# Seven unread matmuls before the first scores, a last product bank by bank with its copy on two engines, and a new issue order

## The chip, the core and the metric

One core of a Trainium2 chip runs the whole kernel. The metric is device time in microseconds of one launch; three runs of the kernel before were timed, and one more execution was profiled.

## What is computed

An attention with pooled keys and values is followed by a gated feed-forward layer. Eight batches of eight heads, 576 positions and head width 64 give 4,608 tokens of width 512; the feed-forward layer has 1,536 hidden columns.

```
k_p, v_p = mean of 8 neighbouring rows of k, v          # 72 keys
attn = softmax(q @ k_p.T / sqrt(64)) ; x = attn @ v_p
out  = (sigmoid(x @ w_gate) * (x @ w_val)) @ w_out
```

## The kernel before

The tokens go through in nine blocks of 512 columns (`BT`). Block 0 goes alone through `first_pass` (L1147); the other eight go in four pairs, and each pair of blocks is multiplied by the weights in seven products of half matrices (a Strassen scheme, `SLOTS`, `product`) instead of eight, first for gate and value (`hidden`), then for the output (`second_sums`, L1069). An operand that needs more than the fast matmul's precision is split into a high and a low part, so that one product is three matmuls (high by high, high by low, low by high).

**Where the order comes from.** No engine runs in the order in which the functions are written. Every call is recorded in `Book` (L283) as a unit, and units that belong together are grouped by `book.unit()`. At the end, L1512 to L1515 issue the recorded units in the order of a table of numbers, `LATER` (L112), one number for each of some 3,800 units. That table alone sets what stands behind what on TensorE (PE), VectorE (DVE), ScalarE (ACT), GpSimd (POOL) and in the queue of transfers (SP). Waits follow from the data and the buffers.

**The start.** `first` (L1165) issues the loads of block 0: keys `k0` to `k3` and queries `q0` to `q3` (one for each pair of heads), the constants, a matrix of ones for summing the values, and the values. POOL zeroes the five key tiles `kbd` (L350 and L356). DVE sums the keys of a pair over eight neighbours (`keys`, L1224), ACT places them in `kbd` (`place_keys`), PE makes the scores (`score_matmuls`, L662), four matmuls for a pair of heads; each is two rows of the trace, because both operands are full 32-bit values. DVE then takes the maximum (`maximum`) and subtracts it (`exps`), ACT takes the exponential, DVE sums, normalises, and PE transposes. The scores rotate through two PSUM banks, tags `sc` and `tp`, and others. DVE also makes a rounded copy `identr` of the identity out of the constants.

**The middle.** Block 0 and the weights' conversion overlap. A weight load (`fetch`, 1,024 KB from `in_wgv`, twelve of them) is turned into 32-bit numbers by ACT (two steps), DVE (two steps), and split by ACT and DVE into `parts` (`to_f32`, L384). PE then works through `chain` products of these parts and `acc` sums.

**The end.** `second_sums` runs 21 units of twelve matmuls (L1091). The last unit, product 4 of the last quarter, adds to two PSUM banks, `c` = 0 and 1: for `k` = 0 three matmuls into bank 0 and three into bank 1, then the same for `k` = 1 (L1105). `result` (L1073) then copies each bank to SBUF in two halves by ACT, and SP sends each half off with a transfer of its own.

Of the kernel before, what the change touches and what calls it, by code (L numbers as in the profile page):

```python
# [11 lines left out]
F32 = mybir.dt.float32  # L12
# [7 lines left out]
P = 128  # L20
# [309 lines left out]
def attention_then_ffn(ctx: ExitStack, tc: tile.TileContext, qT, kT, vm, vr, vn, sums8, wgv, wo, const, out, outT):  # L330
# [738 lines left out]
    def second_sums(n, last, build, later):  # L1069
# [3 lines left out]
        def result(side, half, c, bank, add):  # L1073
# [6 lines left out]
            if last and side and add is None:  # L1080
                for k in (0, BT // 2):
                    nc.scalar.copy(t[:, k:k + BT // 2], bank[:, k:k + BT // 2])
                    nc.sync.dma_start(outT[r:r + P, a + k:a + k + BT // 2], t[:, k:k + BT // 2])
# [486 lines left out]
```

## Time and profile before

| what | value |
|---|---|
| runs | 906.82, 908.58, 909.71 us; median 908.58 |
| profiled execution | 906.58 us, of which the span of the core's instructions is 904.8 |
| PE busy | 891.4 us, 4,148 rows |
| DVE, ACT, POOL busy | 657.4, 544.5, 200.0 us |
| bytes moved | 237.56 MB, mean 263 GB/s |

"Busy" is the time in which an engine has an instruction under way; PE's rows overlap, and a row's length is longer than the distance to the next. The distance is read from the start of one row to the start of the next, or from the length of a merged row and its count.

### The profile page before, as it was taken

How to read it: one execution, taken by the hardware profiler on the slowest of the kernel's cores; microseconds unless marked ns; L12 is line 12 of the kernel's file. 1: busy time of each engine (PE TensorE's matmuls, PEld its weight loads, DVE VectorE, ACT ScalarE, POOL GpSimd, SP SyncE). 2: the span in 40 equal slices, each digit the busy share in tenths (PEclk: the TensorE clock that was granted, in tenths of full speed). 3: DMA queues.
4: the chain of work that ended last, by engine and by line, in shares of the span. 5: the costliest groups of instructions: out<-in, count | busy, mean ns of one | idle time of the engine just before them, and what ended most of it. 6: DMA issues, size and time to landing. Idle time of an engine off the chain costs nothing.

```text
span 904.8 us, 12625 instructions
## 1 busy us (share of the span) xinstructions
PE 891.4 (99%) x4148; PEld 732.7 (81%) x4148; DVE 657.4 (73%) x1038; ACT 544.5 (60%) x1110; POOL 200.0 (22%) x369
## 2 busy tenths in 40 slices
PE   6999999999999999999999999999999999999998
PEld 5788878888888888888888888888888888888886
DVE  7989888889899999756668796355589552224863
ACT  5998998788978476545375555445365552224352
POOL 2422101012164235443443104132213000000000
PEclk9999999999999999999999999999999999999999
DMA  9899888889999888787987877676747776645554
GB/s 337 309 326 336 301 335 298 298 285 338 320 324 316 276 287 286 237 299 259 308 276 237 244 273 264 229 268 194 264 122 252 245 249 207 228 167 204 192 169 143
DMA packets 100433, 237.56 MB, mean 263 GB/s; under 512 B 13872, under 2 KB 34992, under 8 KB 98832
## 3 DMA queue, kind: packets, MB, share of 16 engines
q1 hardware_dynamic: 85328, 203.97, 66.6%
q0 software_dynamic: 15040, 32.79, 10.4%
q8 instruction: 33, 0.54, 0.2%
q14 instruction: 32, 0.26, 0.1%
HBM read 176.02 MB, written 60.69 MB: 262 GB/s over the span
## 4 chain that ended last, share of the span: by engine, by line
PE 81%; ACT 2%; DVE 1%; issue 0%; ACTq 0%
PE chain L317 50%; PE acc L317 25%; PE av L317 3%; PE sc L317 3%; ACT hs L317 0%; DVE s L317 0%; DVE hs L317 0%; PE tp L317 0%; DVE h L317 0%; ACT e L317 0%; ACT L317 0%; ACT raw_o L317 0%; DVE w_o L317 0%; ACT w_o L317 0%; ACT oparts L317 0%
## 5 line engine op out<-in xcount | busy, mean ns | idle before, releaser
L317 PE MATMUL chain<-xo,parts 128*128 128x512 f32 x2316 | 544.1, 392 | 0.5 <-ACT xs L317 0.5
L317 PEld LDWEIGHTS chain<-xo,parts 128*128 128x128 f32 x2316 | 430.7, 188 | 93.3 <-issue 1.0
L317 PE MATMUL acc<-hs,oparts 128*128 128x512 f32 x1008 | 237.0, 391 | 0.2 <-issue 0.2
L317 PEld LDWEIGHTS acc<-hs,oparts 128*128 128x128 f32 x1008 | 188.1, 188 | 40.6 <-DVE hs L317 1.2
L317 POOL DMA_DIRECT2D turned<-turn x240 | 131.7, 551 | 214.3 <-DVE turn L317 184.3
L317 DVE TENSOR_TENSOR y<-chain,sV 128x512 f32<-128x512 f32 x46 | 31.1, 686 | 69.6 <-PE chain L317 54.7
L317 ACT CAST hs<-h 128x1024 fp32r<-128x1024 f32 x52 | 54.3, 1051 | 27.2 <-PE acc L317 22.4
L317 DVE TENSOR_TENSOR hs<-h,hs 128x1024 fp32r<-128x1024 f32 x52 | 63.0, 1217 | 10.5 <-ACT hs L317 10.3
L317 ACT COPY chain<-chain 128x512 f32<-128x512 f32 x46 | 26.5, 577 | 52.8 <-PE chain L317 45.8
L317 DVE TENSOR_TENSOR y<-chain,sG 128x512 f32<-128x512 f32 x46 | 31.2, 682 | 34.2 <-PE chain L317 23.4
L317 ACT CAST hs<-s 128x1024 fp32r<-128x1024 f32 x36 | 37.5, 1050 | 28.5 <-DVE s L317 13.0
L317 DVE TENSOR_TENSOR hs<-s,hs 128x1024 fp32r<-128x1024 f32 x36 | 43.8, 1218 | 11.1 <-ACT hs L317 10.9
L317 ACT COPY sG<-chain 128x512 f32<-128x512 f32 x46 | 26.6, 584 | 41.0 <-PE chain L317 39.4
L317 ACT ACT_TABLE_LOAD x37 | 47.5, 1283 | 0.6
L317 ACT COPY sV<-chain 128x512 f32<-128x512 f32 x46 | 26.7, 584 | 34.0 <-PE chain L317 32.7
L317 ACT ACTIVATE gate<-chain 128x512 f32<-128x512 f32 x46 | 26.9, 594 | 31.8 <-PE chain L317 29.4
L317 DVE TENSOR_TENSOR h<-chain,gate 128x512 f32<-128x512 f32 x46 | 30.7, 679 | 20.1 <-PE chain L317 20.0
L317 PE MATMUL sc<-kbd,raw 128*128 128x144 f32 (+1 forms) x262 | 41.4, 297 | 0.3 <-ACT pr L317 0.2
L317 PEld LDWEIGHTS sc<-kbd,raw 128*128 128x128 f32 (+1 forms) x262 | 33.5, 176 | 8.6 <-issue 2.8
L317 ACT ACTIVATE gate<-y 128x512 f32<-128x512 f32 x46 | 28.9, 632 | 17.0 <-DVE y L317 16.8
L317 PE MATMUL acc<-oparts,hs 128*128 128x512 f32 x144 | 38.7, 402 | 0.0
L317 DVE TENSOR_REDUCE m<-sc 128x4 f32<-128x288 f32 x48 | 21.7, 452 | 17.5 <-PE sc L317 17.2
(210 smaller groups left out, 1099.9 us busy)
## 6 DMA issues: line engine op xcount, KB each, us to landing
oparts<-keptS SPq DMA_DIRECT2D x48, 512.0 KB, 4.7
oparts<-keptO SPq DMA_DIRECT2D x72, 256.0 KB, 4.7
raw<-in_wgv SPq DMA_DIRECT2D x12, 1024.0 KB, 8.1
out<-o SPq DMA_DIRECT2D x34, 256.0 KB, 3.8
raw<-in_kT SPq DMA_DIRECT2D x28, 288.0 KB, 5.0
raw<-in_qT SPq DMA_DIRECT2D x29, 256.0 KB, 4.9
raw<-in_vm SPq DMA_DIRECT2D x24, 256.0 KB, 5.5
raw_o<-in_wo SPq DMA_DIRECT2D x12, 512.0 KB, 8.5
```

The costliest lines, as they stand in the source:

```text
L317: return self._book.take(lambda: f(*args, **named))
```

## The change

1. In `first_pass`, seven matmuls of 128 by 144 with the last key tile (zeroed by POOL, not yet filled) as both operands, into a PSUM tile `idle` that nothing reads.
2. In the last unit of the last pair, bank 0 gets its six matmuls first, then bank 1 its six.
3. In the last `result`, bank 0 is copied whole by ACT and sent with one transfer. Of bank 1, ACT copies the first half and sends it from its own queue, and DVE copies the second half, which SP sends.
4. A new table `LATER`, for all units.

```diff
 LATER = """
-5 4 3 6 0 10 2 7 24 13 17 19 20 8 26 12 27 18 16 30 9 22 21 75 25 34 36 35 46 32 1 44 39 54 38 40 11 29 47 28 51 15 31
...
+6 4 5 0 11 7 2 3 21 18 8 27 28 14 31 20 25 1 19 35 9 13 36 22 23 17 40 48 39 10 26 37 45 76 66 33 32 47 53 67 12 41 30
...
@@ result @@
-            if last and side and add is None:
-                for k in (0, BT // 2):
-                    nc.scalar.copy(t[:, k:k + BT // 2], bank[:, k:k + BT // 2])
-                    nc.sync.dma_start(outT[r:r + P, a + k:a + k + BT // 2], t[:, k:k + BT // 2])
+            if last and side and add is None and c:
+                x, y = slice(0, BT // 2), slice(BT // 2, BT)
+                nc.scalar.copy(t[:, x], bank[:, x])
+                nc.vector.tensor_copy(t[:, y], bank[:, y])
+                nc.scalar.dma_start(outT[r:r + P, a:a + BT // 2], t[:, x])
+                nc.sync.dma_start(outT[r:r + P, a + BT // 2:a + BT], t[:, y])
                 return
@@ second_sums @@
-            for k in range(2):
+            final = last and i + 1 == len(units)
+            for n1 in range(2):
                 with book.unit():
-                    for c in range(2):
+                    for k, c in ((0, n1), (1, n1)) if final else ((n1, 0), (n1, 1)):
...
-                if i == 0 and k == 1:
+                if i == 0 and n1 == 1:
@@ first_pass @@
+        idle = ps.tile([P, HT, 2 * KEYS], F32, name="idle", tag="tp")
+        with book.unit():
+            for _ in range(7):
+                nc.tensor.matmul(idle[:, 0], lhsT=kbd[RING - 1][:, :P], rhs=kbd[RING - 1], start=True, stop=True)
```

**Place 1: DVE and the transfer queue at the start.** These are the first instructions of DVE in the kernel before, each with the semaphores that it waits for; `early<-h` are sums of keys, `early<-sc` maxima of scores, `identr` the rounded identity. Then follow the first transfers on SP.

```order
L317 TENSOR_REDUCE early<-h 128x72 [waits DMAHW0_49]
L317 TENSOR_REDUCE early<-h 128x72 [waits DMAHW1_49]
L317 TENSOR_REDUCE early<-h 128x72 [waits DMAHW3_49]
L317 TENSOR_REDUCE early<-sc 128x4 [waits PE_49]
L317 CAST identr<-cst 128x128 [waits DMAHW4_49]
L317 TENSOR_TENSOR e<-sc,early 128x288 [waits DVE_49]
L317 TENSOR_REDUCE early<-sc 128x4 [waits PE_49]
L317 TENSOR_REDUCE early<-h 128x72 [waits DMAHW6_49]
```

```order
L317 DMA h<-in_kT 128x576 x2
L317 DMA h<-in_qT 128x512
L317 DMA h<-in_kT 128x576
L317 DMA cst<-in_const 128x133
L317 DMA h<-in_qT 128x512
L317 DMA h<-in_kT 128x576
L317 DMA h<-in_qT 128x512
L317 DMA early<-in_qT 128x512
L317 DMA xs_220<-in_sums 128x360
L317 DMA xs_220<-in_vn 64x512
L317 DMA raw_237<-in_wgv 128x2048
```

And the same two in the changed kernel:

```order
L317 TENSOR_REDUCE early<-h 128x72 [waits DMAHW0_49]
L317 CAST identr<-cst 128x128 [waits DMAHW3_49]
L317 TENSOR_REDUCE early<-h 128x72 [waits DMAHW2_49]
L317 TENSOR_REDUCE early<-sc 128x4 [waits PE_49]
L317 TENSOR_TENSOR e<-sc,early 128x288 [waits DVE_49]
L317 TENSOR_REDUCE early<-sc 128x4 [waits PE_49]
L317 TENSOR_REDUCE early<-h 128x72 [waits DMAHW5_49]
```

```order
L317 DMA h<-in_kT 128x576
L317 DMA h<-in_qT 128x512
L317 DMA h<-in_kT 128x576
L317 DMA cst<-in_const 128x133
L317 DMA h<-in_qT 128x512
L317 DMA h<-in_kT 128x576 x2
L317 DMA xs_220<-in_vn 64x512
L317 DMA h<-in_qT 128x512
L317 DMA xs_220<-in_sums 128x360
L317 DMA raw_238<-in_wgv 128x2048
L317 DMA early<-in_qT 128x512
```

On DVE the third sum of keys moved behind the first two maxima, and the rounded identity moved ahead of the second sum. On SP the first queries moved up by one place, and the fourth queries (`early<-in_qT`) moved behind the first weight load.

**Place 2: the transfer queue at the last four weight loads** (about 100 us into the kernel). First the kernel before, then the changed one; `keptO` and `keptWO` are stores of converted output weights, `raw_o` loads of output weights, 512 KB each.

```order
L317 DMA raw_368<-in_wgv 128x2048 [waits DMAHW3_49,DMAHW7_49,DMAHW0_49,PE_49]
L317 DMA raw_371<-in_wgv 128x2048 [waits DMAHW4_49,DVE_49]
L317 DMA raw<-in_vm 128x512 [waits DMAHW5_49,DVE_49]
L317 DMA raw<-in_kT 128x576 [waits DMAHW6_49]
L317 DMA keptO_193<-oparts 128x1024 [waits DVE_49]
L317 DMA keptO_192<-oparts 128x1024
L317 DMA raw_381<-in_wgv 128x2048 [waits DMAHW3_49,DMAHW1_49,DVE_49]
L317 DMA keptWO_201<-w_o 128x1024 [waits DMAHW2_49]
L317 DMA raw_383<-in_wgv 128x2048 [waits PE_49]
```

```order
L317 DMA raw_369<-in_wgv 128x2048 [waits DMAHW4_49,DMAHW6_49,DMAHW0_49,PE_49]
L317 DMA raw_o<-in_wo 128x1024 [waits DMAHW5_49,DVE_49]
L317 DMA raw_372<-in_wgv 128x2048
L317 DMA keptO_192<-oparts 128x1024 [waits DMAHW7_49,DVE_49]
L317 DMA raw_o<-in_wo 128x1024
L317 DMA keptWO_201<-w_o 128x1024 [waits DMAHW1_49]
L317 DMA raw_382<-in_wgv 128x2048 [waits DMAHW4_49,DMAHW2_49,DVE_49]
L317 DMA keptO_193<-oparts 128x1024 [waits DMAHW3_49]
L317 DMA raw_384<-in_wgv 128x2048 [waits PE_49]
```

Two loads of output weights and one store moved ahead of the third weight load; values, keys and one store moved away from there.

**Place 3: the last instructions of ACT, DVE and SP.** In the kernel before, ACT and then SP end with

```order
L317 COPY o<-acc 128x256 [waits DVE_49,PE_49]
L317 COPY o<-acc 128x256
L317 COPY o<-acc 128x256 [waits PE_49]
L317 COPY o<-acc 128x256
```

```order
L317 DMA out<-o 128x256 [waits DMAHW1_49,Activation_49]
L317 DMA out<-o 128x256 [waits DMAHW2_49,Activation_49]
L317 DMA out<-o 128x256 [waits DMAHW3_49,Activation_49]
L317 DMA out<-o 128x256 [waits DMAHW4_49,Activation_49]
```

In the changed kernel ACT, then DVE, then SP end with

```order
L317 COPY o<-acc 128x512 [waits DVE_49,PE_49]
L317 COPY o<-acc 128x256 [waits PE_49]
L317 DMA out<-o 128x256 [waits DMAHW2_49,Activation_49]
```

```order
L317 COPY o<-acc 128x256 [waits DMAHW1_49,Activation_49,Pool_49]
```

```order
L317 DMA out<-o 128x512 [waits DMAHW1_49,Activation_49]
L317 DMA out<-o 128x256 [waits DMAHW3_49,DVE_49]
```

DVE's half of the last copy has a wait for ACT and none for PE.

## Rows read from the trace of the kernel before

**Rows 1.** The page: the span; busy time, share of the span and rows of each engine.
```profile
span 904.8 us, 12625 instructions
...
PE 891.4 (99%) x4148; PEld 732.7 (81%) x4148; DVE 657.4 (73%) x1038; ACT 544.5 (60%) x1110; POOL 200.0 (22%) x369
```

**Rows 2.** Stretches of the span: start and end, length, busy time (and rows) of each engine, granted PE clock, DMA share, GB/s.
```profile
5.50:20.60 15.10, 13.13 (x68) 10.92 (x68) 13.81 (x37) 8.91 (x23) 1.03 (x1) 1.00 1.04 376
...
27.50:900.80 873.30, 871.41 (x4047) 717.39 (x4045) 635.50 (x989) 527.38 (x1073) 192.42 (x343) 1.00 0.77 260
```

**Rows 3.** The waits of PE between 27.5 and 901 us: waiting engine, line and tile, what it waited for, us in total, times, longest.
```profile
PE tp L317 <- ACT y L317: 0.5, 1, 0.5
PE chain L317 <- ACT xs L317: 0.5, 1, 0.5
```

**Rows 4.** Timeline of PE at the start: start us, length us, instruction, count of rows, in brackets the idle time before and what ended it.
```profile
5.51 4.33 PE L317 MATMUL sc<-kbd,h 128*128 128x144 f32 x16 [5.51 <-DMA h<-in_qT]
10.02 1.22 PE L317 MATMUL sc<-kbd,h 128*128 128x144 f32 x8 [0.18 <-issue]
...
12.43 1.60 PE L317 MATMUL sc<-kbd,early 128*128 128x144 f32 x8
14.95 0.55 PE L317 MATMUL tp<-cst,early 128*128 128x128 f32 x3 [0.91 <-DVE early L317]
...
20.66 0.63 PE L317 MATMUL tp<-cst,early 128*128 128x128 f32 x4 [0.56 <-DVE r L317]
```

**Rows 5.** Timeline of POOL, ACT and DVE at the start, same columns; the last row is of the grouped view of DVE from 5 to 30 us (count, busy us, mean ns).
```profile
0.78 0.83 POOL L318 MEMSET kbd<- 128x144 f32 x5
...
4.57 0.53 ACT L317 ACTIVATE kbd<-early 64x72 f32<-64x72 f32 x2 [2.33 <-DVE early L317]
...
6.66 0.75 DVE L317 TENSOR_REDUCE early<-h 128x72 f32<-128x576 f32 x1 [1.46 <-DMA h<-in_kT]
7.33 0.45 DVE L317 TENSOR_REDUCE early<-sc 128x4 f32<-128x288 f32 x1
7.69 0.22 DVE L317 CAST identr<-cst 128x128 fp32r<-128x128 f32 x1
7.82 0.45 DVE L317 TENSOR_TENSOR e<-sc,early 128x288 f32<-128x288 f32 x1
...
11.04 0.74 DVE L317 TENSOR_REDUCE early<-e 128x8 f32<-128x576 f32 x1
...
L317 DVE TENSOR_TENSOR vres<-vr,vres 32x128 fp32r<-32x128 f32 x4 | 1.2, 290 | 0.1
```

**Rows 6.** Transfers at the start: when SP issued them (timeline of SP), and three of them with size in KB and us from issue to landing.
```profile
2.60 0.43 SPq L317 DMA_DIRECT2D cst<-in_const  x1
...
4.50 0.43 SPq L317 DMA_DIRECT2D early<-in_qT  x1
...
6.65 0.33 SPq L317 DMA_DIRECT2D raw<-in_wgv  x1
...
cst<-in_const SPq DMA_DIRECT2D x1, 66.5 KB, 4.2
...
early<-in_qT SPq DMA_DIRECT2D x1, 256.0 KB, 5.2
...
raw<-in_wgv SPq DMA_DIRECT2D x1, 1024.0 KB, 7.0
```

**Rows 7.** Around the last four weight loads: the first and the third with the time from issue (99.7 and 110.0 us) to landing; the stretch from 100 to 130 us (columns as in rows 2); ACT, DVE and PE in their timelines.
```profile
raw<-in_wgv SPq DMA_DIRECT2D x1, 1024.0 KB, 4.9
...
raw<-in_wgv SPq DMA_DIRECT2D x1, 1024.0 KB, 7.9
...
100.00:130.00 30.00, 29.14 (x149) 23.38 (x148) 25.26 (x46) 28.75 (x78) 2.85 (x6) 1.00 0.98 357
...
117.94 1.14 ACT L317 ACTIVATE w<-raw 128x1024 f32<-128x1024 f32 x1 [0.78 <-DMA raw<-in_wgv]
...
123.04 0.60 ACT L317 ACTIVATE y<-chain 128x512 f32<-128x512 f32 x1
...
123.17 1.29 DVE L317 TENSOR_TENSOR parts<-w,parts 128x512 fp32r<-128x512 f32 x2
...
124.58 4.77 PE L317 MATMUL chain<-xo,parts 128*128 128x512 f32 x20
```

**Rows 8.** The end: timelines of PE, ACT and SP, and the last transfer's size and time to landing.
```profile
897.62 3.11 PE L317 MATMUL acc<-hs,oparts 128*128 128x512 f32 x13
...
900.09 1.33 ACT L317 COPY o<-acc 128x256 f32<-128x256 f32 x4 [6.86 <-PE acc L317]
...
901.88 0.39 SPq L317 DMA_DIRECT2D out<-o  x1
...
out<-o SPq DMA_DIRECT2D x1, 128.0 KB, 1.8
```

**Rows 9.** Prices for what the trace has not: ACT's copies of a bank or half of one (least, middle and largest ns), a DVE subtraction that reads a whole bank, a DVE maximum over 288 columns of a bank (count, busy us, mean ns), and the transfers that POOL issues (count, busy us, mean ns of one, idle before).
```profile
L317 ACT COPY o<-acc x6: 372/379/589, 879.5 to 901.0; 128x256 f32<-128x256 f32 x4, 128x512 f32<-128x512 f32 x2
...
L317 DVE TENSOR_TENSOR o<-acc,sG x2: 684/688/691, 883.5 to 891.5; 128x512 f32<-128x512 f32 x2
...
L317 DVE TENSOR_REDUCE early<-sc 128x4 f32<-128x288 f32 x8 | 3.5, 446 | 0.0
...
L317 POOL DMA_DIRECT2D turned<-turn x240 | 131.7, 551 | 214.3 <-DVE turn L317 184.3
```

308 rows, old and new, of the table LATER are left out of this document.

## The prediction

> **What bounds the kernel now.** I read the page's busy shares first, then the stretches, PE's waits, and the timelines of both ends. The page says PE: 891.4 of 904.8 us [rows 1]. The stretches say where the rest is. From 27.5 to 900.8 us PE is busy for 871.41 of 873.30 us [rows 2], so 1.89 us is all the idle time that a new order could win in 97% of the kernel, and the two longest waits in it are 0.5 us each [rows 3]. In the start, 5.50 to 20.60 us, it is DVE that is full: 13.81 of 15.10 us, against 13.13 for PE [rows 2]. DVE waits there 1.46 us for the third keys, until 6.66, and then its rows follow each other, while PE waits for DVE at 14.95 (0.91 us) and at 20.66 (0.56 us) [rows 4, 5]. After the second of these PE hardly waits again. So a sooner end needs one of three things: DVE earlier in the start, fewer waits in the middle, or a shorter end after the last matmul.
>
> **The seven matmuls.** The program's eight score matmuls of two pairs of heads are 16 rows in the trace, so seven are 14 rows. [...] At 0.271 the 14 rows take 3.8 us. The zeroed tile that they need is there at 0.78 + 0.83 = 1.6 us [rows 5], so they end at 5.4. The first scores were held until 5.51 by their queries [rows 4], which are one transfer earlier now; their keys are placed at 4.57 + 0.53 = 5.10 [rows 5]. So the unread rows delay the scores by at most 0.3 us against what would be possible, and not at all against 5.51.
>
> What they can give: with PE at the fast level from the first scores, 16 × (0.271 − 0.153) = 1.9 us of PE time. The trace has no kernel with work this early, so the bounds are 0 (the level rises as late as before) and 1.9. But this time lies beside DVE's. DVE took its first maximum at 7.33, behind a sum of keys, not behind the scores.
>
> [...]
>
> **The start by DVE's order.** In the changed order DVE does one sum of keys, the rounded identity, a second sum, and then the first maximum. The identity waits for the constants. They were issued at 2.60 and took 4.2 us, landing at 6.8 [rows 6]; now one transfer of 288 KB fewer is ahead of them, 0.8 us at the 376 GB/s of this stretch [rows 2], so 6.0. From there: identity 0.13 (7.69 to 7.82), sum 0.67 (6.66 to 7.33), first maximum at 6.8 instead of 7.33 [rows 5]. From the maximum to the first sum of exponentials (11.04) there were 3.71 us; the new order has a sum of keys more (0.67) and the identity less (0.13), 4.25, so 11.05. Nothing is gained, as the same work stands in a row; were the constants there 0.4 us sooner, 0.4 would be. Before the transpose at 20.66 one more `vres` step (0.29 [rows 5]) stands in the new order.
>
> On SP the fourth queries now stand behind the first weight load. They landed at 4.50 + 5.2 = 9.7; that load at 6.65 + 7.0 = 13.65 [rows 6]. With 256 KB less before it the load lands near 12.95 and the queries behind it near 13.65. PE, ready for these scores at 12.43, waits 1.2 us and then needs 8 × 0.153 = 1.2, to 14.85. What stands behind them on PE waits for DVE until 14.95 anyway [rows 4], so the wait is covered by 0.1; each us later costs one.
>
> The start together: −0.4 to 0 from the constants, +0.29, 0 to +0.6 from the queries. I take 0, between −0.5 and +0.7.
>
> **The middle.** All units are moved, the products themselves not. I take 0. The lower bound is −1.89, all idle time gone. For the upper, the place with least slack is the third of the last four weight loads. It took 7.9 us to land where the first took 4.9; ACT waited 0.78 us for it until 117.94, was full until it made `y` at 123.04, for which PE waited 0.5, and DVE finished the parts at 124.46 for PE's products at 124.58 [rows 3, 7]. The new SP row has, between the first load and the third, four transfers of 512 KB (place 2) where there were two and values and keys of 256 and 288 KB: 2,048 KB against 1,568, so 480 more, 1.4 us at 357 GB/s [rows 7]. ACT and DVE took 6.5 us from the landing to the parts, much of it other work. So the upper bound is about +1.4, with PE idle that long.
>
> **The end.** PE's last row ends at 897.62 + 3.11 = 900.73 [rows 8]. Before, four half copies and four transfers followed, each transfer behind the other in one queue: the last was issued at 901.88, though the last copy ended at 901.42, and landed 1.8 us later [rows 8]. Now bank 0 is ready six matmuls (6 × 0.23 = 1.4 us) before the end; its copy of 0.59 [rows 9] is done at 899.9 and its transfer is hidden. ACT's half of bank 1 ends at 900.76 + 0.38 = 901.14. DVE's half waits for ACT (place 3), so the two do not run side by side. DVE has no copy of 256 columns of a bank here; 344 ns (half of the 688 of 512 columns) and 446 (288 columns) [rows 9] bound it, and I take 0.40, so 901.6, and SP issues at 901.65. That is 0.23 before 901.88. ACT issues its own transfer at 901.2; the trace has no transfer issued by ACT, the nearest are SP's 0.39 and POOL's 0.551 us [rows 8, 9], and either is covered by the 0.45 to 901.65. I take −0.25, between −0.7 (side by side) and +0.3 (an issue on ACT that costs 0.7 more than SP's).
>
> [...] Side by side the end would give −0.7, in a row −0.25.
>
> **The sum.** 906.58 + 0 + 0 − 0.25 = 906.33 for the profiled execution, which lies 2.0 below the median of the runs. On the median: 908.58 − 0.25 = **908.3 us**. The terms' bounds make 905.5 to 910.7, all ends together.
>
> **The rivals.**
> - *The scores pull DVE with them.* If the fast scores let DVE fill its idle 1.46 us before 6.66 [rows 5], the start gives −1.46: 906.9. For it: the keys' third sum moved behind the first maxima. Against: the identity ahead of the second sum, on transfers that are not ready.
> - *The order is better all along.* The start's 1.46, the middle's 1.89 and the end's 0.7: 904.5. Against: the waits are small and scattered, and the new order has its own.
> - *A late weight load stops PE (slower).* At the third load a lag of 7.9 − 4.9 = 3.0 us, as this one had, comes on top of 1.14 us (as at 117.94) for a conversion of output weights that ACT now makes before the third load's parts; ACT, in order, passes both on, and PE has no slack at 124.58 [rows 7]: 908.3 + 4.1 = 912.4. It decides from the point at which the load lands over 1.4 us later than 117.9. For it: ACT waited for this load already. Against: an ACT step on which PE waited stands ahead of it now.
> - *The clock doesn't rise sooner.* Then the first term is 0 as in the forecast: 908.3.
>
> **How the numbers follow.** About 0.3%, 2.7 us, is what a measurement of this kernel can tell from no change. Forecast with the unchanged clock 0.62 (own range 906.3 to 910.3), DVE pulled along 0.09, better order 0.15, late load 0.14. Faster than 905.9: the better order and a little of the second, 0.18; slower than 911.3: the late load, 0.14; the rest 0.68. The range takes in the better order and the terms' upper bounds, and leaves out most of the late load: 904.4 to 910.9.
>
> **What would show it.** Right: 14 rows on `idle` from 1.6 to 5.4 us; scores at 0.15 each from the first or second pair on; DVE's first maximum near 6.8 and its first sum of exponentials near 11.0; PE's transpose of 20.66 within 0.7 us of that; idle PE of 1 to 3 us from there to the end; DVE's last copy after ACT's; last transfer issued near 0.9 us after PE's last row, where it was 1.15. Wrong: that transpose over 1 us earlier or later, PE idle for over 3 us around 125 us, or the two last copies side by side.

## The result: 0.7% slower, where no change was forecast

| | before | changed |
|---|---|---|
| median of the runs | 907.8 us (4 runs) | 914.79 us (4 runs, 912.73 to 915.34) |
| profiled execution, and its span | 906.58, 904.8 | 914.49, 912.7 |
| first chain product starts on PE | 27.52 | 28.98 |
| PE's last row ends | 900.73 | 908.89 |
| from there to the end of the span | 4.07 | 3.81 |

The ratio is 1.007, with a 95% interval from 1.0046 to 1.0095. The spans differ by 7.9 us: 1.46 before the first chain product, 6.70 between it and PE's last row (879.91 for 873.21), and −0.26 behind that row. The forecast had 0, 0 and −0.25.

**Page and stretches of the changed kernel**, columns as in [rows 1] and [rows 2].

```profile
span 912.7 us, 12677 instructions
...
PE 897.3 (98%) x4162; PEld 734.6 (80%) x4162; DVE 658.0 (72%) x1039; ACT 543.6 (60%) x1108; POOL 203.8 (22%) x369
```

```profile
5.50:20.60 15.10, 10.45 (x65) 9.06 (x66) 14.15 (x34) 8.52 (x20) 1.46 (x1) 1.00 1.05 387
...
27.50:908.90 881.40, 876.93 (x4055) 718.31 (x4053) 636.00 (x990) 527.35 (x1072) 196.78 (x344) 1.00 0.77 258
80.00:100.00 20.00, 18.14 (x79) 14.31 (x78) 13.29 (x20) 12.64 (x22) 7.29 (x8) 0.91 0.82 303
...
92.10:95.40 3.30, 3.30 (x9) 2.56 (x9) 2.44 (x5) 0.00 (x0) 0.88 (x3) 0.50 1.01 407
```

From 27.5 us on PE is idle for 4.47 us; in [rows 2] it was 1.89. These 2.58 us are less than half of the 6.70; the rest stands in the trace as longer busy time of PE. One place stands out, 80 to 100 us: PE idle for 1.86, and a granted clock of 0.91, because in the stretch from 92.1 to 95.4 it was 0.50. There only nine rows of PE lie in 3.3 us, where the kernel before has 19 at a granted 1.00. The view of waits of PE from 27.5 us names the place:

```profile
PE sc L317 <- POOL kbd L317: 1.9, 1, 1.9
PE acc L317 <- ACT ph L317: 0.6, 1, 0.6
PE chain L317 <- ACT chain L317: 0.5, 1, 0.5
```

**That place in the timelines** of POOL, DVE and PE of the changed kernel:

```profile
85.33 1.22 POOL L317 TENSOR_SCALAR kbd<-early 64x72 f32<-64x72 f32 x1 [20.44 <-DVE early L317]
86.64 0.86 POOL L317 TENSOR_SCALAR vres<-other,cst 96x64 fp32r<-96x64 f32 x2
87.59 3.56 POOL L317 TENSOR_SCALAR kbd<-early 64x72 f32<-64x72 f32 x1
...
87.95 1.20 DVE L317 TENSOR_TENSOR hs<-h,hs 128x1024 fp32r<-128x1024 f32 x1
89.08 0.67 DVE L317 TENSOR_TENSOR parts<-w,parts 128x512 fp32r<-128x512 f32 x1
89.69 1.21 DVE L317 TENSOR_TENSOR oparts<-w_o,oparts 128x1024 fp32r<-128x1024 f32 x1
...
91.20 1.01 PE L317 MATMUL sc<-kbd,raws 128*128 128x144 f32 x6 [1.86 <-POOL kbd L317]
...
92.44 4.34 PE L317 MATMUL chain<-xo,parts 128*128 128x512 f32 x12
```

POOL places a key tile in two halves. In the order before they stood together (83.25 us, 0.90 us for both); in the new one two `vres` steps stand between them. The second half took 3.56 us, an operation that takes 0.38 elsewhere, and ended just after DVE's row of three operations, each of which reads two SBUF tiles. Its own row begins 0.36 us before that of `hs`, and still `hs` went first. PE waited for it, and then ran slowly: twelve chain rows in 4.34 us.

**The start** in the timelines of PE, DVE and POOL, beside [rows 4] and [rows 5]:

```profile
1.67 3.73 PE L317 MATMUL idle<-kbd 128*128 128x144 f32 x14 [1.67 <-POOL kbd L318]
5.22 1.97 PE L317 MATMUL sc<-kbd,h 128*128 128x144 f32 x8
7.59 1.25 PE L317 MATMUL sc<-kbd,h 128*128 128x144 f32 x8 [0.40 <-ACT kbd L317]
...
16.95 0.33 PE L317 MATMUL tp<-cst,pm 128*128 128x128 f32 x1 [0.90 <-DVE pm L317]
...
22.21 0.52 PE L317 MATMUL tp<-cst,early 128*128 128x128 f32 x3 [0.77 <-DVE r L317]
...
6.83 0.45 DVE L317 TENSOR_REDUCE early<-sc 128x4 f32<-128x288 f32 x1
...
11.58 0.74 DVE L317 TENSOR_REDUCE early<-e 128x8 f32<-128x576 f32 x1
...
14.76 0.69 DVE L317 TENSOR_TENSOR early<-e,early 128x512 f32<-128x512 f32 x1
15.36 1.53 DVE L317 TENSOR_TENSOR pm<-e,early 128x512 f32<-128x512 f32 x1
...
14.89 1.46 POOL L317 TENSOR_SCALAR w<-w 128x1024 f32<-128x1024 f32 x1 [11.71 <-ACT w L317]
```

DVE is 0.54 late at its first sum of exponentials and loses 0.84 more at `pm`, which took 1.53 for the 0.69 of its neighbour of the same shape: POOL's step on the weights lay across it. Here POOL waited for one operation only: its step begins inside `early<-e,early`, took 1.46 us (1.03 in both fixes, below) and ran ahead of `pm`, though `pm` follows without a pause. The transposes of 20.66 in [rows 4] come at 22.21.

**The end**, beside [rows 8], in the timelines of PE, ACT, DVE:

```profile
900.45 8.44 PE L317 MATMUL acc<-hs,oparts 128*128 128x512 f32 x36
...
908.92 0.37 ACT L317 COPY o<-acc 128x256 f32<-128x256 f32 x1 [0.77 <-PE acc L317]
...
909.38 0.42 DVE L317 COPY o<-acc 128x256 f32<-128x256 f32 x1 [6.09 <-issue]
```

Here all went as foreseen: DVE's half behind ACT's.

**Where the rest lies.** I lined up PE's rows of two traces by the units of the table (the rows on one tile name, in issue order, against that order's units) and took how much later each matmul starts than in the trace before, as a median over stretches of 25 us of that trace:

| stretch starts at | 25 | 50 | 75 | 100 | 150 | 225 | 300 | 450 | 875 us |
|---|---|---|---|---|---|---|---|---|---|
| changed kernel, late by | 1.5 | 2.2 | 2.8 | 6.1 | 5.3 | 6.2 | 6.6 | 7.1 | 8.2 |

So the start costs 1.5, the stretch up to 75 us 1.3 more, the place at 90 us 3.3, and what follows 150 us 2.9, in small steps; 0.8 comes back between 100 and 150 us.

### The profile page after: what moved, and what is told of

It is laid out like the page before. It is cut to its first block, busy times and chain, and to the rows that moved or that the text cites. A ratio compares the mean times of both kernels' runs of the same rounds, so it can differ in the third digit from the quotient of the medians.

```text
span 912.7 us, 12677 instructions
## 1 busy us (share of the span) xinstructions
PE 897.3 (98%) x4162; PEld 734.6 (80%) x4162; DVE 658.0 (72%) x1039; ACT 543.6 (60%) x1108; POOL 203.8 (22%) x369
## 4 chain that ended last, share of the span: by engine, by line
PE 74%; ACT 6%; DVE 5%; issue 2%; DMA 1%; ACTq 0%; DVEq 0%
PE chain L317 45%; PE acc L317 23%; PE av L317 3%; PE sc L317 3%; ACT e L317 1%; DMA pt<-turned 1%; DVE s L317 1%; ACT L317 1%; ACT hs L317 1%; DVE h L317 1%; DVE parts L317 1%; DVE hs L317 1%; DMA h<-keptwV 0%; ACT parts L317 0%; DVE early L317 0%
```

## The experiments

All are compared with the kernel before on the same chip. Theory 1 was: the order alone costs the time, at the three places above. Its rival: the unread matmuls do, through the clock.

| run | median, us | ratio to before, 95% | first chain product |
|---|---|---|---|
| old order, new parts | 907.69 | 0.9997 [0.9987, 1.0006] | 27.27 |
| new order, old parts | 914.28 | 1.0071 [1.0056, 1.0085] | 30.69 |
| put up | 914.25 | 1.0077 [1.0063, 1.0091] | 28.36 |
| old start, new rest | 912.41 | 1.0054 [1.0039, 1.0068] | 27.64 |
| ACT places | 911.35 | 1.0044 [1.0032, 1.0056] | 28.79 |
| POOL behind pm | 914.62 | 1.0076 [1.006, 1.0091] | 31.17 |
| both fixes | 910.01 | 1.0032 [1.002, 1.0043] | 27.82 |
| gap in DVE's row | 912.32 | 1.0049 [1.0034, 1.0064] | 29.66 |
| queries up | 910.05 | 1.0027 [1.0015, 1.004] | 28.33 |
| old to 770 units, then new | 914.84 | 1.0081 [1.0068, 1.0094] | 27.45 |
| old to 714 units, then new | 910.96 | 1.0034 [1.0024, 1.0044] | 27.75 |
| both fixes to 714 units, then old | 920.71 | 1.0133 [1.0111, 1.0155] | 27.51 |

### Order and parts taken apart

```diff
 LATER = """                               (old order, new parts: the order before, numbered for the new unit 2)
-6 4 5 0 11 7 2 3 21 18 8 27 28 14 31 ...
+6 5 4 7 0 11 2 3 8 25 14 18 20 21 9 ...
 LATER = """                               (new order, old parts: on the kernel before)
-5 4 3 6 0 10 2 7 24 13 17 19 20 8 26 ...
+5 3 4 0 10 6 2 20 17 7 26 27 13 30 ...
```

> The changed kernel with the order of before: the seven unread matmuls and the new end stay, every other unit stands where it stood. Theory 1 (the new order alone costs the time, the parts give only the end's 0.26 us): 907.5, ratio 0.9997, one granted-clock rise near 7 us, no wait over 0.6 us after 27.5. Rival (the unread matmuls cost it, since a clock that rises sooner falls later): 911 to 915, with a stretch of granted 0.5 somewhere in the middle.

> The kernel before with the new order and nothing else: no unread matmuls, the old end. Theory 1: 915.0 (1.5 us late at the first chain product, 3.5 us around 90 us, some 3 us in many places, end as before). Rival (the matmuls cost it): 908 to 909, no fall of the clock near 92 us.

Theory 1 holds for both: the parts change nothing that can be measured, the order alone costs the 0.7%. The stretch of granted 0.5 that the rival foresaw does not show: in the old order with the new parts the granted clock has a mean of 1.00 in every stretch of the view from 30 to 898 us. But in the new order the unread matmuls are not without effect. Without them its first chain product comes at 30.69, 1.7 us later than with them, since PE stayed slow for longer in the start: eight score rows at 10.78 us, behind a wait of 1.30, took 2.26 us, which take 1.22 in the changed kernel. The granted clock is 1.00 from 10 to 20 us in that trace, so it does not show what slowed them. These are single executions. Three more runs below have this start and the unread matmuls, and their first chain products lie at 28.36 to 29.66, so the gain is 1.0 to 2.3 us. Its timeline around 90 us has the same wait, and no slow rows behind it:

```profile
92.59 1.00 PE L312 MATMUL sc<-kbd,raws 128*128 128x144 f32 x6 [1.86 <-POOL kbd L312]
...
93.66 2.88 PE L312 MATMUL chain<-xo,parts 128*128 128x512 f32 x12
```

Twelve chain rows take 2.88 us here and 4.34 in the changed kernel. So in the new order the unread matmuls won 1.7 us in the start of the profiled execution, and 1.9 were lost again (879.91 for 878.02 from the first chain product to PE's last row), 1.46 of it in those twelve rows. In the old order they move the first chain product by 0.25.

### The late key tile

```diff
-... 523 489 514 525 ... 469 470 490 468 ...   (put up)
+... 523 489 490 514 525 ... 469 470 468 ...
```

> The changed kernel with one number of the table moved: the second half of the key tile placed by POOL at 87.59 us goes to right behind its first half, ahead of two vres steps, as in the order before. Theory 1 (POOL came to it while DVE had a row of operations and was kept out for 3.56 us, PE then waited 1.86 us and its clock fell): 914.8 - 3.5 = 911.3, no wait of PE on kbd there, no granted 0.5 near 92 us. Rival (a late key tile is covered, PE was ahead and would wait for the next thing): 914.5, with another wait of about 2 us within the next 10 us.

The rival held. The tile was in time, and now a `vres` step was late. POOL and PE in their timelines:

```profile
84.45 1.70 POOL L312 TENSOR_SCALAR kbd<-early 64x72 f32<-64x72 f32 x2 [20.16 <-DVE early L312]
86.24 4.08 POOL L312 TENSOR_SCALAR vres<-other,cst 96x64 fp32r<-96x64 f32 x2
...
90.38 0.47 PE L312 MATMUL av<-other,vres 96*128 96x448 f32 x1 [2.80 <-POOL vres L312]
```

DVE's row ran from 87.06 to 90.01 here, and POOL ended at 90.32. So the tile's place alone was not what cost. Theory 2: POOL had one operation too many ahead of a row of DVE that keeps it out. It is tested from two sides:

```diff
-                if j:                                    (ACT places)
+                if j and (j, p) != (2, 0):
                     nc.gpsimd.tensor_scalar_mul(out=t[r, c], ...)
                 else:
                     nc.scalar.activation(t[r, c], ...)
```

> The changed kernel with ACT instead of POOL placing the one key tile on which PE waits at 91.20 us (two copies of 64 by 72). Theory 2 (POOL has three small operations to do before DVE's row of hs, parts and oparts, and the one that comes too late is kept out for the whole row, whichever it is: moving the tile up only passed the wait on to vres, 2.80 us): with the tile on ACT, POOL has only two vres steps there, of 0.4 us each, PE's wait of 1.86 us is gone, so is the granted 0.5 at 92 us with its 1.7 us; 914.6 - 3.5 = 911.1. Rival (the new order is short of DVE's work itself there): a wait of 1.5 to 3 us stays between 88 and 98 us, on DVE or ACT, 914 to 915.

```diff
-... 519 503 552 536 541 509 352 542 ...   (gap in DVE's row; DVE's numbers alone)
+... 519 352 503 552 536 541 509 542 ...
```

> The changed kernel with one number moved on DVE: a sum of keys that stands at 93.36 us goes between hs and parts, into DVE's row of three operations with two SBUF inputs each, so that the same work follows in another order. It reads one SBUF tile only. Theory 2 (POOL's small step is let in at the first DVE operation that does not read two SBUF tiles): POOL's kbd row, 3.56 us, ends during that sum, near 89.5, so 1.8 to 2.0 us long; PE's wait of 1.86 us shrinks to 0.1 to 0.3, no granted 0.5 behind it, 914.6 - 1.7 - 1.9 = 911.0. Rival (POOL's row is long for DMA traffic or of itself): POOL's row stays over 3 us, 914.6.

With the tile on ACT: 911.35, as theory 2 had it (911.1), no wait there, and a granted 1.00 from 92 to 95 us. The gap shows how POOL is kept out, in the timelines of POOL, DVE and PE:

```profile
87.92 1.82 POOL L312 TENSOR_SCALAR kbd<-early 64x72 f32<-64x72 f32 x1
89.83 2.37 POOL L312 TENSOR_SCALAR vres<-other,cst 96x64 fp32r<-96x64 f32 x1
...
88.28 1.20 DVE L312 TENSOR_TENSOR hs<-h,hs 128x1024 fp32r<-128x1024 f32 x1
89.41 0.73 DVE L312 TENSOR_REDUCE early<-raw 128x72 f32<-128x576 f32 x1
90.08 0.67 DVE L312 TENSOR_TENSOR parts<-w,parts 128x512 fp32r<-128x512 f32 x1
90.67 1.21 DVE L312 TENSOR_TENSOR oparts<-w_o,oparts 128x1024 fp32r<-128x1024 f32 x1
...
89.18 1.61 PE L312 MATMUL sc<-kbd,raws 128*128 128x144 f32 x8
...
90.86 2.92 PE L312 MATMUL chain<-xo,parts 128*128 128x512 f32 x12
```

POOL got in during the sum, which reads one SBUF tile: 1.82 us (1.8 to 2.0 expected). Its next step was kept out again until the end of `oparts`. PE had no idle time there and its chain rows were fast. From the first chain product to PE's last row this execution takes 876.16 us, 3.7 less than the changed kernel, and theory 2 had 3.6. The total, 912.32, is 1.3 above what I expected; this execution's first chain product came late, at 29.66. In its start DVE's `rest` took 1.11 us for 0.28 beside POOL's weights step, and from 16.6 to 19.9 us the granted clock was 0.50; what each of these costs no run separates.

One part of theory 2 does not hold in general: that POOL is let in at the first DVE operation that does not read two SBUF tiles. With the tile on ACT and in both fixes (below) POOL's first `vres` step comes earlier. POOL, then DVE, in the timelines of both fixes:

```profile
79.54 3.75 POOL L312 TENSOR_SCALAR vres<-other,cst 96x64 fp32r<-96x64 f32 x1 [15.81 <-DVE other L312]
...
79.53 1.21 DVE L312 TENSOR_TENSOR hs<-h,hs 128x1024 fp32r<-128x1024 f32 x1
80.66 1.21 DVE L312 TENSOR_TENSOR oparts<-w_o,oparts 128x1024 fp32r<-128x1024 f32 x1
81.80 0.67 DVE L312 TENSOR_REDUCE early<-early 96x64 f32<-96x512 f32 x1
82.39 0.67 DVE L312 TENSOR_SCALAR w_o<-w_o 128x1024 f32<-128x1024 f32 x1
```

It ended at 83.29, behind a sum and a step on `w_o`, both with one SBUF input. PE did not wait for it, as it came early enough. In the kernel before, too, a `vres` step took 0.95 for 0.44 beside such a step on `w_o`; POOL, then DVE:

```profile
84.24 0.95 POOL L317 TENSOR_SCALAR vres<-other,cst 96x64 fp32r<-96x64 f32 x1
...
84.28 0.69 DVE L317 TENSOR_SCALAR w_o<-w_o 128x1024 f32<-128x1024 f32 x1 [0.38 <-ACT w_o L317]
```

Why one sum let POOL in and the other did not, the runs do not show.

The traces show that one keeps the other out: at 90 us a POOL operation that takes 0.38 us elsewhere took 3.56 and sat out three DVE instructions; at 15 us POOL's step took 1.46 us for 1.03 and sat out one of two, and the second, `pm`, took 1.53 us for 0.69. What decides between the two no run here shows.

### The start

```diff
@@ first units @@                          (old start, new rest)
-6 4 5 0 11 7 2 3 21 18 8 27 28 14 31 ...
+6 5 4 7 0 11 2 3 8 25 14 18 20 21 9 ...   (155 units in the old order, the others in the new)
```

> The changed kernel with its first units in the order of before, up to PE's first chain product (the first 155 units, plus the unread matmuls), then the new order for all that is left. Theory 1: the start's 1.5 us come back, 913.3, first chain row at 27.5. Rival (what the start loses is waited for later anyway, by weights that arrive at the same time): 914.8, with waits on weights or keys before 130 us that the changed kernel does not have.

The first chain product came at 27.64, as theory 1 had it, and the interval holds the 913.3. The other costs stayed: PE waited 1.8 us on `kbd`, so what the start lost is not waited for later anyway.

```diff
     book.open = False                                         (POOL behind pm)
+    book.units[84][0].behind = book.units[85][0]
-... 98 137 84 72 88 85 79 ...
+... 98 137 72 88 85 84 79 ...
```

> The changed kernel with one wait added: POOL's first step of the weights (at 14.89 us) waits for DVE's pm, which it lay beside. Theory 2 (the two exclude each other: pm took 1.53 us for 0.68 because POOL had begun first): pm takes 0.68 us, the transposes that came at 22.21 come at 21.4, the first chain product at 28.1 for 28.98, 913.7 to 914. Rival (pm was long for another reason, or the weights' step is what the first chain product waits for): pm stays at 1.5 us or the first chain product stays at 29.0 or later, 914.6.

> The two edits together, the key tile on ACT and POOL's step behind pm. Theory 2: 914.6 - 3.5 - 0.85 = 910.2. What would then be left over the kernel before, 2 to 2.5 us, are the new order's short waits behind 100 us and 0.65 us of its start. Rival (waits pass on): over 913.

The wait alone settles nothing: `pm` took 0.69 us, but POOL's step came only at 17.16 in that execution, released by ACT and not by the wait, and PE ran at a granted 0.50 from 11 to 21 us; the first chain product came at 31.17. In both fixes together POOL's step was held by `pm`, as meant, and `pm` took 0.69. DVE, POOL and PE in the timelines:

```profile
14.97 0.69 DVE L312 TENSOR_TENSOR pm<-e,early 128x512 f32<-128x512 f32 x1
...
15.85 1.03 POOL L312 TENSOR_SCALAR w<-w 128x1024 f32<-128x1024 f32 x1 [12.68 <-DVE pm L312]
...
27.82 1.43 PE L312 MATMUL chain<-xo,parts 128*128 128x512 f32 x5
```

910.01 for the expected 910.2. The step from the tile on ACT alone is 1.3 us, more than the 0.85 of `pm`; the granted clock, 0.50 from 14.6 to 17.8 us in that run's execution and 1.00 from 5.5 to 20.6 in this one, may have a part in it. With the tile on ACT alone the same collision took another form: POOL's step began earlier, at 14.40, and DVE's operation ahead of `pm` was the long one, 1.52 us.

```diff
-... 3 21 18 8 27 28 14 31 20 25 ...   (queries up, on both fixes; 8 and 25 are the third and fourth queries)
+... 3 21 8 18 27 28 14 31 25 20 ...
```

> The kernel with both fixes (key tile on ACT, POOL behind pm) and two transfers moved up on SP: the third queries before a load of values, the fourth queries before the first weight load. PE's waits for them (1.1 and 1.4 us) go. Theory 2 (DVE bounds the start, so these waits are covered): 909.5 to 910.0, first chain product at 27.6 to 27.9. Rival (each late query delays the start): 908.5, first chain product at 26.8 or earlier.

910.05: PE's waits for queries went, waits on the key tiles and on DVE took their place, and the time is that of both fixes. The late queries were covered. The first chain product, at 28.33, came later than the 27.6 to 27.9 that I expected.

### What lies behind 116 us

```diff
-LATER = new order                                        (old to 770, old to 714)
+LATER = the order before, its first 770 (714) units; then what is left, in the new order
```

> The order of before for the first 770 units, that is to about 125 us, then the new order for the rest, with the unread matmuls and the new end. Theory 2 (some 2.5 us of the 7 lie behind 130 us, as PE's idle time of 130 to 300 us, 1.24 us for 0.13, and somewhat longer spacing): 907.8 + 2.5 = 910.3. Rival (behind 130 us the new order is as good, and what looks longer there follows from the delay before): 907.5 to 908.2.

> As the run with the order of before for the first 770 units, but cut at 714 units (about 116 us), where the two orders have all but 3 units in common, so that the joint itself should cost nothing. Theory 2: what lies behind 116 us costs 2 to 2.5 us, 910. Rival: nothing behind 116 us costs, 907.7.

```diff
-LATER = new order, both fixes                            (both fixes to 714, then old)
+LATER = its first 714 units; then what is left, in the order before
```

> The kernel with both fixes up to the same cut at 714 units, then the order of before. Theory 2 (both fixes repair the start and the 90 us place; 2 us are lost behind 116 us): 910.0 - 2.0 = 908.0, no different from before. Rival (the 2.3 us that are left lie ahead of 116 us): 910.

The times of two of the three tell nothing of the orders: the joint made a wait that neither order has. In the first and the third, PE's waits from 110 to 150 us:

```profile
PE chain L312 <- ACT parts L312: 3.5, 1, 3.5
```

```profile
PE chain L312 <- ACT early L312: 6.5, 1, 6.5
```

The second has a joint without such a wait, and its ratio lies 0.0037, or 3.4 us, above that of the old order with the new parts. By the lining up of rows, it is 2.0 late at 150 us and 4.8 at 875; both fixes 0.6 and 2.9, the changed kernel 5.3 and 8.2. So the new order loses 2.3 to 2.9 us behind 150 us in each of them, whatever happened before. Of the 2.0 in the second run, 1.8 came at 96 to 103 us, where its order is still the one of before (the old order with the new parts loses 1.2 there), so its 3.4 us are not the new order's alone. Behind the joint the other two do tell something: with the new order the first run is 6.6 late at 150 us and 9.2 at 875, with the old one the third is 8.8 and 9.1. One wait of it has a name and stands in all three, 0.5 us at about 180 us (PE chain <- ACT chain). For the rest I found only spacing, a few tenths at a time. A single execution of the old order with the new parts lost 1.1 us to the trace before at about 275 us, so part of the 2.3 to 2.9 may be the luck of that trace. The old order behind 150 us thus loses 0.3 and 1.1, the new one 2.3 to 2.9; which waits make the difference stays open.

## Why the prediction was wrong

- **Unread matmuls.** Their 14 rows lie at 1.67 to 5.40 us (1.6 to 5.4 foreseen), the scores began at 5.22, not later, and the second pair ran at 0.156 a row. The 0.271 and 0.153 us a row that the prediction reckons with are 4.33 us by 16 and 1.22 by eight [rows 4], the second of them what it calls the fast level; the granted clock was 1.00 beside both [rows 2], so that view does not show what sets them apart. That the gain is covered by DVE was right in the old order (0.25 us). In the new one they saved 1.7 in the one pair of traces, of a loss that the new order itself had brought.
- **DVE's start.** The constants (6.03 for 6.0) and the first maximum (6.83 for 6.8) came as worked out; the first sum of exponentials at 11.58 for 11.05, 0.29 of it a wait for keys. What failed is the term for all that follows, 0 with a bound of +0.7: the transposes came 1.55 later, one of the signs of being wrong that the prediction named. (Its three parts, −0.4 to 0, +0.29 and 0 to +0.6, add up to −0.1 to +0.9, not to the −0.5 to +0.7 beside them; 1.55 is outside both.) I counted DVE's own instructions with their durations and did not ask what POOL does beside them; 0.84 us are POOL's weights step across `pm`.
- **Queries.** PE waited 1.42 us for the fourth, 1.2 foreseen, and it was covered.
- **The middle: the step that failed.** "I take 0", between −1.89 and +1.4, with 6.70 measured. The bound came from one place, the third weight load, where nothing happened (PE idle for 0.61 us from 100 to 130 us; 0.86 in [rows 7]). I named no work queued on POOL, though its order was to be read: two `vres` steps between the halves of a key tile, ahead of DVE's row. That place cost 3.3 us: 1.86 the wait, 1.46 the slow chain rows behind it. And I took a table that moves every unit as neutral on average; its small losses behind 150 us came to 2 or 3 us more, part of which may be scatter.
- **The end.** −0.26 for −0.25: DVE's half 0.42 us for 0.40, SP's last transfer 0.95 us behind PE's last row for 0.9. Whether the two halves could run side by side, for the −0.7 of the lower bound, no run shows.
- **The sum.** On 908.58 the upper bounds add up to 911.0, not 910.7; the measured 914.79 lies above either.
- **The rivals.** Slower had 0.14, by a late weight load. The side was right, the mechanism was not: the transfers were in time, and an engine off the path was kept from its work by another.

## What to carry to other kernels

When a table moves every instruction of a kernel in which PE hardly waits, zero is the best case and not the middle: compare, on each engine, what stands between an operation and its consumer, and on POOL what DVE runs at that moment. Here a POOL step of 0.38 us, on whose result PE waited 1.86 us, took 3.56 us beside a row of three DVE operations with two SBUF inputs each; with that key tile on ACT the wait was gone, and the median was 911.35 us for 914.79. So look, in a kernel's own trace, for short POOL operations on whose result PE waits and that take several times as long as elsewhere, and try them on another engine. And before moving a late operation forward, see what it pushes back: here a `vres` step, on which PE then waited 2.80 us.

## What the runs showed of the hardware

- In these traces DVE and POOL kept each other out: 3.56 us for one POOL step of 0.38 us, 4.08 for two and 2.37 for one of 0.44, all behind DVE, and 1.53 us for DVE's 0.69 behind POOL. POOL sat out three DVE operations in a row at 90 us, and four at 79.54 us in both fixes. Not all of these have two SBUF inputs: beside a step on `w_o` with one, POOL's 0.44 us became 0.95 (kernel before, 84.24 us). A sum, with one input too, let POOL in in the run with the gap (1.82 us) and not at 81.80 us in both fixes (3.75 us).
- A wait of PE of 1.8 to 2.8 us in the middle of full work, near 90 us, stands in five traces: the changed kernel and the new order with the old parts (1.86 each), put up (2.80), old start (1.8) and POOL behind `pm` (1.9). In the changed kernel and in put up the granted clock was 0.50 for 3.3 us behind it (92.1 to 95.4 and 92.0 to 95.3 us); in old start its mean from 80 to 100 us was 0.91, as in those two; in the new order with the old parts it was 1.00 from 93.6 to 96.9. Twelve chain rows behind the wait took 4.34 us in the changed kernel and 2.88 there, and the whole way from the first chain product to PE's last row 1.9 us more. The mean granted clock varies from run to run: 0.992 to 0.998 in the changed kernel's four, 0.998 to 1.000 in the runs of the kernel before that were compared.
- With work for PE before its first scores the score rows were fast sooner: the second pair's took 0.156 us each at 7.59 us, where the kernel before took 0.271 until 9.84, both at a granted 1.00. PE did not stay fast in every trace with the unread matmuls. The granted clock was 0.50 from 11 to 21 us in POOL behind `pm`, where PE had waited 2.0 us for queries until 11.21; it was 0.50 from 14.6 to 17.8 us with the tile on ACT and from 16.6 to 19.9 in the run with the gap, and its mean from 5.5 to 30 us was 0.93 in old start.
